# One VectorE operation for the sum of two accumulators and its relu in a seven-product matrix multiplication

## The chip, the core and the metric

The kernel runs on one core of a Trainium2 chip. The metric is the device time of one execution in microseconds (us). The core's engines work side by side, each through its own list of instructions in order: TensorE (PE in the profile, its weight loads PEld), VectorE (DVE), ScalarE (ACT), GpSimd (POOL) and SyncE (SP). They wait for one another by semaphores.

## The reference, cut to what matters

Two layers follow each other: an attention with a squared relu in place of the softmax, over 8 batches, 12 heads, 448 positions and a head size of 64, and then a feed-forward block over the 3584 tokens with width 768 and inner width 2048.

```python
scores = scale * np.matmul(q, k.transpose(0, 1, 3, 2))
attn = np.maximum(scores, 0.0) ** 2 / S
x = np.matmul(attn, v)            # 8 x 448 tokens, 768 wide after the heads are put together
h = x @ w_in                      # 768 -> 2048
g = np.maximum(h, 0.0) ** 2
out = g @ w_out                   # 2048 -> 768
```

## The kernel before, in words

Matrices are fp16 in SBUF, sums are fp32 in PSUM. The batches are taken in four pairs (`pr` 0 to 3). For each pair the kernel makes the attention output `xt`, from it `h` and the squared relu `g`, and from `g` the output. The attention of a later pair is spread in small pieces through the matrix multiplications of an earlier one.

**h, first pair** (batches 0 and 1): plain products, `h_group`, line 414. **h, later pairs** (batches 2 to 7): seven products in place of eight, after Winograd's form of Strassen's method, `h_period`, line 471. A batch is done in two periods (`i0` 0 and 4), so there are 12 periods. A period has two streams `s` of products; the list `order` (lines 528 to 542) gives the 14 products of a period, and beside each what is to be done with its accumulator when its last matmul is issued:

- `copy` (line 486): ScalarE copies an accumulator from PSUM to an fp32 tile in SBUF (`m1`, `m5`, `u2`, `u3`).
- `plus` (line 491): VectorE adds an accumulator in PSUM and such a tile, and writes an fp16 quarter of `g`, 128 partitions x 448 elements. There are 6 in a period, 72 in all (line 493).
- `relu21` (line 502): ScalarE takes the relu of one accumulator into the left half of an upper block of `g`; the right half had been written by `plus`. Then `rest`.
- `c12` (line 506): the last `plus` of a lower block of `g`. Then `rest`.
- `rest` (line 495): puts two VectorE operations on the list `due_g`: a relu in place over what `plus` had written (after `relu21` the right half, 448 elements; after `c12` the whole block, 896 elements; line 498), and the square of the whole block (line 500).

**The output**: `o_groups`, line 610, again by seven products, each of 8 matmuls of 128x384 (line 739), for two rows of tokens at a time. Four of the products take as left operand a sum of parts of `g` that VectorE makes beforehand: `sums`, line 598, `s1` to `s4` (line 608). `s1` and `s2` of the first group are made in the last period of `h` (line 897); `s3` is asked for when the third product ends (`end6`, line 663) and used by the fifth.

**The order of the work.** PE's order is laid down by the list `steps` and by `events`, which bring in pieces of attention (`visit`, line 373) at times of a clock `clock` that adds up the steps' costs (lines 916 to 930). VectorE's order is chosen by a small planner: `at_pe` and `at_ve` are its estimates of how far PE and VectorE are. `due` holds squares of attention tiles, `due_g` the operations of `rest`; each entry has a time from which it may run and a cost. `now_ve` adds the cost of an operation that is issued at once. `fill(until)` issues entries, `due` first, as long as they end by `until`:

```python
def put(d):
    ready, cost, fn, _ = d.popleft()
    at_ve[0] = max(at_ve[0], at_pe[0], ready) + cost
    fn()

def fill(until):
    for d in (due, due_g):
        while d and max(at_ve[0], at_pe[0], d[0][0]) + d[0][1] <= until:
            put(d)
```

`fill` is called at the end of each product in `h` (line 562) and in the output (line 749). `flush_g` (line 365) issues everything on `due_g` up to a batch; it stands ahead of the sums. In the output the entries left over that the next group needs are shared out over the first four products: after product `k` the rounded-up share `some / (4 - k)` of those that are left (lines 745 to 748). The planner's clocks are read by these places alone: neither PE's list nor ScalarE's is ordered by them.

Of the kernel before, what the change touches and what calls it, by code (L numbers as in the profile page):

```python
# [9 lines left out]

# [3 lines left out]
ALU = mybir.AluOpType  # L14
# [3 lines left out]
def kernel(  # L18
# [9 lines left out]
    nc = tc.nc  # L28
# [315 lines left out]
    at_pe = [0.0]  # L344
# [12 lines left out]
# [5 lines that stand above are left out]
    def now_ve(cost, lag=0.25):  # L362
        at_ve[0] = max(at_ve[0], at_pe[0] + lag) + cost
# [38 lines left out]
    def mm_tile(i=None, dtype=FP32):  # L402
        if i is None:
            mm_no[0] += 1
            i = mm_no[0] % len(big)
        return big[i].tile(
            [P, 2048 // mybir.dt.size(dtype)], dtype, name="mm", tag="mm")

    def g_of(b):
        if b // 2 not in gts:  # L410
            gts[b // 2] = g_p.tile([P, NF, 2 * S], FP16, name="g", tag="g")
        return gts[b // 2]
# [58 lines left out]
    def h_period(b, i0, extra):  # L471

        z = (b % 2) * S
        XY = [[None, None], [None, None]]
        keep: dict = {}

        def gs(s, hi, right=None):
            f = i0 + 2 * s + (8 if hi else 0)
            c = (slice(z, z + S) if right is None
                 else slice(z + Q, z + S) if right else slice(z, z + Q))  # L480
            return g_of(b)[:, f:f + 2, c]

        def acc(s, y):
            return XY[s][y][:, 0:S].rearrange("p (r c) -> p r c", r=2)

        def copy(s, y, nm, tag):
            t = late["m"].tile([P, S], FP32, name=nm, tag=tag)
            nc.scalar.activation(out=t, in_=XY[s][y][:, 0:S], func=AF.Copy)
            keep[s, nm] = t.rearrange("p (r c) -> p r c", r=2)

        def plus(s, y, nm, hi, right):
            now_ve(0.54)
            nc.vector.tensor_add(gs(s, hi, right), acc(s, y), keep[s, nm])  # L493

        def rest(g, relu, lag):

            t = at_pe[0] + lag
            due_g.append((t, 0.32 if relu is g else 0.2, lambda: nc.vector.tensor_scalar(  # L498
                out=relu, in0=relu, scalar1=0.0, scalar2=None, op0=ALU.max), b))
            due_g.append((t, 0.54, lambda: nc.vector.tensor_mul(g, g, g), b))  # L500

        def relu21(s):
            nc.scalar.activation(out=gs(s, True, False), in_=acc(s, 0), func=AF.Relu)
            rest(gs(s, True), gs(s, True, True), 0.8)

        def c12(s):
            plus(s, 1, "u2", False, True)
            g = gs(s, False)
            rest(g, g, 0.0)

        def left(k, f, m):

            c, n = f // 4, slice((f % 4) * P, (f % 4 + 1) * P)
            if k in (1, 2):
                return w1[c][:, m + NH * (k - 1), n]
            if k in (4, 7):
                return w1[c + 2][:, m + (NH if k == 4 else 0), n]
            return wsum[{5: 0, 6: 1, 3: 2}[k], c][:, m, n]

        def right(k, m):  # L520
            if k in (1, 2):
                return xts[b][:, m + NH * (k - 1), 0:Q]
            if k in (3, 7):
                return xts[b][:, m + (NH if k == 3 else 0), Q:S]
            return xsum[b, {5: 0, 6: 1, 4: 3}[k]][:, m]


        order = (
            (0, 1, 0, True, lambda: copy(0, 0, "m1", "a")),
            (1, 1, 0, True, lambda: copy(1, 0, "m1", "b")),  # L530
            (0, 2, 1, True, lambda: plus(0, 1, "m1", False, False)),
            (0, 6, 0, False, lambda: copy(0, 0, "u2", "c")),
            (1, 6, 0, False, lambda: copy(1, 0, "u2", "d")),
            (1, 2, 1, True, lambda: plus(1, 1, "m1", False, False)),
            (0, 5, 1, True, lambda: copy(0, 1, "m5", "a")),
            (0, 7, 0, False, lambda: plus(0, 0, "m5", True, True)),
            (1, 7, 0, False, lambda: copy(1, 0, "u3", "b")),
            (1, 5, 1, True, lambda: plus(1, 1, "u3", True, True)),
            (0, 4, 0, False, lambda: relu21(0)),
            (1, 4, 0, False, lambda: relu21(1)),  # L540
            (0, 3, 1, False, lambda: c12(0)),
            (1, 3, 1, False, lambda: c12(1)))

        FREE = {2: 0.6, 5: 0.6, 7: 0.1, 9: 0.6, 12: 0.6, 13: 1.0, 16: 0.6}

        def step(p, r, m):
            s, k, y, fresh, end = order[p]

            def run():
                if fresh and r == 0 and m == 0 and k != 5:  # L550
                    XY[s][y] = mm_tile(s)
                nc.tensor.matmul(  # L552
                    XY[s][y][:, r * Q:(r + 1) * Q],
                    lhsT=left(k, i0 + 2 * s + r, m), rhs=right(k, m),
                    start=(fresh and r == 0 and m == 0), stop=(m == NH - 1),
                    skip_group_check=not (fresh and r == 0))
                if r == 1 and m == NH - 1:
                    end()
                    for fn in extra.get(p, ()):
                        fn()  # L560
                    nx = min(n for n in FREE if n > p)
                    fill(at_pe[0] + (nx - p) * 0.576 + 0.25 + FREE[nx])
            return run

        return [(0.096, step(p, r, m), r == 0 and m == 0 and p not in (0, 1, 6, 8))
                for p in range(14) for r in range(2) for m in range(NH)]
# [393 lines left out]
```

## Time and profile before

| what | value |
|---|---|
| median of 8 runs | 374.06 us (373.76 to 374.51) |
| the profiled execution: its own time | 374.36 us |
| its span, from the first to the last instruction | 372.6 us |
| VectorE busy | 279.2 us (75%), 518 instructions |
| ScalarE busy | 247.7 us (66%), 370 instructions |
| relus of line 498 | 24 of 896 elements, mean 388 ns; 24 of 448, mean 289 ns |
| squares of line 500 | 48 of 896 elements, mean 622 ns |
| sums of line 493 | 72 of 448 elements, mean 620 ns |

A line of the timeline gives the start in us from the span's start, a duration, the engine, the line of the code, the operation with the tile that it writes and those that it reads, the shapes, and how many like it were merged; in brackets stands the idle time before it and what ended that. `mm` is an accumulator in PSUM; `s` is one of the sums `s1` to `s4`; `at` is an attention tile. An instruction's duration is longer than the time that it takes on its engine when the next one is waiting: two squares of attention tiles in a row, each of 0.62 us, are shown merged as 1.15 to 1.16 us. The time that an instruction takes in a full queue is therefore read from start to start.

The stages of the second to fourth pair: `h` from about 121 to 167 us, 210 to 257 and 294 to 331; the output in between and from 331 us to the end. In the 35 us from 296 to 331 VectorE was busy for 29.91 us, ScalarE for 22.04 and PE for all 35.00.

### The profile page before, as it was taken

Reading aid. Unit: us, or ns where it says so; the run is one execution under the profiler, and the core shown is the slowest. Engines: PE = TensorE matmul, PEld = TensorE weight load, DVE = VectorE, ACT = ScalarE, POOL = GpSimd, SP = SyncE. Lnnn points to the kernel's source line nnn. Section 1 sums busy time; section 2 is a strip of 40 time slices with the busy share of each in tenths; the row PEclk is TensorE's granted clock in tenths of the full one; section 3 lists DMA queues with packets and bytes.
Section 4 is the critical chain, followed back from the end, with each engine's and each line's share of the span. In section 5 each row is a group of like instructions: output and inputs, shape, how many; then the busy total and the mean of one; then the engine's idle time right before and its main releaser. Section 6 shows DMA issues by size and latency. Waiting matters only on the chain.

```text
span 372.6 us, 8794 instructions
## 1 busy us (share of the span) xinstructions
PE 361.9 (97%) x3600; PEld 230.8 (62%) x3600; DVE 279.2 (75%) x518; ACT 247.7 (66%) x370; POOL 107.4 (29%) x128
## 2 busy tenths in 40 slices
PE   7889999999999999999999999999999999999994
PEld 3544444445555778885555588786455689975653
DVE  1897677996766887798975668989956688995442
ACT  2997895786667999876556588886665885532220
POOL 8545421747433455522053145140000000000001
PEclk9999999999999999999999999999999999999999
DMA  8999999999999999978799999491233300002333
GB/s 116 199 204 205 205 204 151 122 159 125 206 171 151 174 94 114 113 97 70 132 131 113 187 154 95 79 120 31 52 84 87 86 0 2 2 0 74 95 90 83
DMA packets 121159, 42.64 MB, mean 114 GB/s; under 512 B 100832, under 2 KB 117760, under 8 KB 121120
## 3 DMA queue, kind: packets, MB, share of 16 engines
q0 software_dynamic: 82912, 23.01, 62.0%
q1 hardware_dynamic: 38048, 18.98, 26.8%
q8 instruction: 28, 0.46, 0.5%
q10 hardware_dynamic: 160, 0.10, 0.1%
q14 instruction: 11, 0.09, 0.1%
HBM read 45.61 MB, written 11.01 MB: 152 GB/s over the span
## 4 chain that ended last, share of the span: by engine, by line
PE 84%; DVE 7%; ACT 5%; issue 2%; DMA 1%; POOL 0%; POOLq 0%; DVEq 0%; ACTq 0%
PE mm L739 31%; PE mm L552 25%; PE mm L422 9%; PE slot L254 9%; PE slot L319 7%; ACT at L258 4%; DVE at L371 2%; DMA k<-in_k_dram 1%; DVE s L608 1%; DVE g L500 1%; PE slot L225 1%; DVE g L493 1%; DVE xt L285 1%; DVE osb L646 1%; DVE g L498 1%
## 5 line engine op out<-in xcount | busy, mean ns | idle before, releaser
L258 ACT ACTIVATE at<-slot 128x896 f16<-128x896 f32 x168 | 145.9, 919 | 28.4 <-PE slot L254 28.4
L371 DVE TENSOR_TENSOR at<-at 128x896 f16<-128x896 f16 x168 | 99.1, 619 | 11.1 <-ACT at L258 11.0
L108 POOL DMA_DIRECT2D qs<-in_q_dram x36 | 35.5, 987 | 113.3 <-DMA qT<-qs 106.1
L739 PEld LDWEIGHTS <-s 128*128 128x128 f16 x440 | 41.3, 98 | 34.2 <-DVE s L608 3.8
L254 PE MATMUL slot<-qT,kT 64*64 64x448 f16 x756 | 57.4, 360 | 1.6 <-ACT at L258 0.9
L552 PEld LDWEIGHTS <-w 128*128 128x128 f16 x576 | 54.3, 98 | 5.2 <-issue 4.3
L552 PE MATMUL mm<-xt,w 128*128 128x224 f16 x432 | 49.0, 259 | 0.0
L739 PEld LDWEIGHTS <-g 128*128 128x128 f16 x336 | 31.7, 98 | 24.1 <-issue 4.7
L552 PEld LDWEIGHTS <-ws 128*128 128x128 f16 x432 | 40.3, 98 | 4.7 <-issue 4.7
L739 PE MATMUL mm<-b,g 128*128 128x384 f16 x224 | 40.7, 326 | 0.0
L739 PE MATMUL mm<-b,s 128*128 128x384 f16 x216 | 39.6, 327 | 1.0 <-DVE s L608 0.9
L422 PE MATMUL mm<-xt,w 128*128 128x448 f16 x192 | 39.8, 354 | 0.0
L646 DVE SCALAR_TENSOR_TENSOR osb<-mm,u 128x384 f32<-128x384 f32 (+1 forms) x30 | 16.2, 543 | 31.1 <-ACT u L641 19.2
L739 PE MATMUL mm<-t,s 128*128 128x384 f16 x224 | 39.4, 326 | 0.0
L108 POOL DMA_DIRECT2D ks<-in_k_dram x36 | 35.2, 978 | 12.3 <-DMA b<-in_moe_w_out_dram 5.8
L254 PEld LDWEIGHTS <-kT 64*64 64x64 f16 x756 | 19.6, 104 | 28.9 <-issue 23.9
L575 POOL DMA_DIRECT2D out_dram<-osb x2 | 1.1, 565 | 121.0 <-DVE osb L646 121.0
L641 ACT ACTIVATE u<-mm 128x384 f32<-128x384 f32 x28 | 13.8, 492 | 32.5 <-PE mm L739 31.3
L552 PE MATMUL mm<-x,ws 128*128 128x224 f16 x288 | 34.1, 259 | 0.0
L319 PE MATMUL slot<-at,vt 64*64 64x448 f16 x588 | 31.9, 350 | 0.2
L500 DVE TENSOR_TENSOR g<-g 128x896 f16<-128x896 f16 x48 | 29.8, 622 | 1.2
L493 DVE TENSOR_TENSOR g<-mm,m 128x448 f16<-128x448 f32 x36 | 22.2, 620 | 10.2 <-PE mm L552 7.0
(69 smaller groups left out, 394.9 us busy)
## 6 DMA issues: line engine op xcount, KB each, us to landing
out_dram<-osb SPq DMA_DIRECT2D x52, 192.0 KB, 3.2
vt<-in_v_dram POOLq DMA_DIRECT2D x24, 224.0 KB, 6.5
qs<-in_q_dram POOLq DMA_DIRECT2D x36, 112.0 KB, 4.7
ks<-in_k_dram POOLq DMA_DIRECT2D x36, 112.0 KB, 5.3
w<-in_moe_w_in_dram POOLq DMA_DIRECT2D x8, 384.0 KB, 11.6
b<-in_moe_w_out_dram POOLq DMA_DIRECT2D x4, 768.0 KB, 18.0
q<-in_q_dram POOLq DMA_DIRECT2D x6, 224.0 KB, 7.7
k<-in_k_dram POOLq DMA_DIRECT2D x6, 224.0 KB, 8.2
```

What stands on the lines that cost most here:

```text
L108: nc.gpsimd.dma_start(out=t[:, :, hh, :], in_=heads(src, n)[:, hh].rearrange("p (j d) -> p j d", d=D))
L254: nc.tensor.matmul(ps[c, hh, 0:S], lhsT=kT[r, j, c], rhs=qT[r, :, c], start=True, stop=True)
L258: nc.scalar.activation(out=at, in_=ps[:, :, 0:S], func=AF.Relu, scale=SK)
L319: nc.tensor.matmul(ps[64 * hh:64 * hh + 64, hp, 0:S], lhsT=vt[r, hh, j * D:(j + 1) * D], rhs=at[r, hh, :], start=(j == 0), stop=(j == J - 1))
L371: lambda: nc.vector.tensor_mul(at, at, at), 0))
L422: nc.tensor.matmul(cell[0][:, 0:S], lhsT=w1[f // 4][:, m, (f % 4) * P:(f % 4 + 1) * P], rhs=xts[b][:, m, :], start=(m == 0), stop=(m == NM ...
L493: nc.vector.tensor_add(gs(s, hi, right), acc(s, y), keep[s, nm])
L500: due_g.append((t, 0.54, lambda: nc.vector.tensor_mul(g, g, g), b))
L552: nc.tensor.matmul(XY[s][y][:, r * Q:(r + 1) * Q], lhsT=left(k, i0 + 2 * s + r, m), rhs=right(k, m), start=(fresh and r == 0 and m == 0), ...
L641: nc.scalar.activation(out=t, in_=X[0][:, 0:HALF], func=AF.Copy, scale=CO)
L646: nc.vector.scalar_tensor_tensor(out=osb[row][:, c], in0=acc[0][:, 0:cc.stop - cc.start], scalar=CO, in1=keep[nm][:, cc], op0=ALU.mult, op ...
L739: nc.tensor.matmul(acc[0][:, 0:HALF], lhsT=left()[:, f], rhs=right[:, f], start=(fresh and f == 0), stop=(f == KH - 1), skip_group_check=n ...
```

## The change

`plus` is no longer a plain addition but one VectorE operation that adds, takes the smaller of the sum and 3.4e38, and takes the larger of that and 0: sum and relu at once. As every value that `plus` writes has then had its relu, `rest` puts only the square on `due_g`. The estimated cost of `plus` in the planner stays 0.54, that of the square too; the entries for the relu, of 0.2 and 0.32, are gone.

```diff
+from concourse.dve_ops import TENSOR_ADD_SAT
...
         def plus(s, y, nm, hi, right):
+
             now_ve(0.54)
-            nc.vector.tensor_add(gs(s, hi, right), acc(s, y), keep[s, nm])
-
-        def rest(g, relu, lag):
-
-            t = at_pe[0] + lag
-            due_g.append((t, 0.32 if relu is g else 0.2, lambda: nc.vector.tensor_scalar(
-                out=relu, in0=relu, scalar1=0.0, scalar2=None, op0=ALU.max), b))
-            due_g.append((t, 0.54, lambda: nc.vector.tensor_mul(g, g, g), b))
+            nc.vector._custom_dve(
+                TENSOR_ADD_SAT, out=gs(s, hi, right), in0=acc(s, y),
+                in1=keep[s, nm], s0=3.4e38, s1=0.0)
+
+        def rest(g, lag):
+            due_g.append((at_pe[0] + lag, 0.54,
+                          lambda: nc.vector.tensor_mul(g, g, g), b))
 
         def relu21(s):
             nc.scalar.activation(out=gs(s, True, False), in_=acc(s, 0), func=AF.Relu)
-            rest(gs(s, True), gs(s, True, True), 0.8)
+            rest(gs(s, True), 0.8)
 
         def c12(s):
             plus(s, 1, "u2", False, True)
-            g = gs(s, False)
-            rest(g, g, 0.0)
+            rest(gs(s, False), 0.0)
```

## Prediction

> **What bounds the kernel now.** I read the page first: the span, the engines' busy time and the clock.
>
> ```profile
> span 372.6 us, 8794 instructions
> PE 361.9 (97%) x3600; PEld 230.8 (62%) x3600; DVE 279.2 (75%) x518; ACT 247.7 (66%) x370; POOL 107.4 (29%) x128
> PEclk9999999999999999999999999999999999999999
> ```
>
> PE is busy nearly throughout, at the full clock. VectorE, the only engine that the change touches, has 93 us of idle time in the span. So its busy time is not what the change can save; only places where PE stands still for VectorE are. The second view is therefore the waits of PE from 121 us on, where the seven products of h begin. It has one line:
>
> ```profile
> PE mm L739 <- DVE s L608: 0.9, 2, 0.7
> ```
>
> PE's matmuls waited twice for a sum `s` of VectorE, 0.9 us together, 0.7 the longer. The third view, PE's timeline, shows where:
>
> ```profile
> 261.50 1.47 PE L739 MATMUL mm<-t,s 128*128 128x384 f16 x8
> 263.69 1.47 PE L739 MATMUL mm<-b,s 128*128 128x384 f16 x8 [0.72 <-DVE s L608]
> ```
>
> The bracket counts from the modelled end of the matmul before; what is lost is more. Eight matmuls of this shape that follow each other without a wait take 1.30 us from start to start (337.44 to 338.74 in the same view). The second group was therefore due at 261.50 + 1.30 = 262.80 and came at 263.69: **0.89 us lost**. The other place is the same product of the last pair: 16 such matmuls start at 333.19, the next product was due at 335.79 and came at 336.13: **0.34 us lost**. A further group came late at 207.63 (due 204.66 + 2.60 = 207.26, lost 0.37), behind attention squares that waited for ScalarE; the last relu before it is at 184.7, so the change doesn't reach it. The groups at 130.91 (0.13) and 290.91 (0.2) were late for ScalarE's tiles, not for VectorE's.
>
> The fourth view is VectorE's own timeline ahead of the first of these places:
>
> ```profile
> 257.38 0.38 DVE L498 TENSOR_SCALAR g<-g 128x896 f16<-128x896 f16 x1
> 257.68 0.62 DVE L493 TENSOR_TENSOR g<-mm,u 128x448 f16<-128x448 f32 x1
> 258.21 0.68 DVE L608 TENSOR_TENSOR s<-s,g 128x1024 f16<-128x1024 f16 x1
> 258.81 0.62 DVE L500 TENSOR_TENSOR g<-g 128x896 f16<-128x896 f16 x1
> 259.35 0.27 DVE L498 TENSOR_SCALAR g<-g 128x448 f16<-128x448 f16 x1
> 259.72 0.62 DVE L500 TENSOR_TENSOR g<-g 128x896 f16<-128x896 f16 x1
> 260.27 0.55 DVE L646 SCALAR_TENSOR_TENSOR osb<-mm,m 128x384 f32<-128x384 f32 x1
> 260.73 0.27 DVE L498 TENSOR_SCALAR g<-g 128x448 f16<-128x448 f16 x1
> 261.03 0.63 DVE L500 TENSOR_TENSOR g<-g 128x896 f16<-128x896 f16 x1
> 261.58 0.39 DVE L498 TENSOR_SCALAR g<-g 128x896 f16<-128x896 f16 x1
> 261.88 1.16 DVE L371 TENSOR_TENSOR at<-at 128x896 f16<-128x896 f16 x2
> 262.95 0.69 DVE L608 TENSOR_TENSOR s<-g 128x1024 f16<-128x1024 f16 x1
> ```
>
> No line has a bracket: from 255.77 on VectorE is a full queue, and the sum that PE waits for is its last line. PE's matmul starts 0.74 us after that sum (263.69 - 262.95). Four of the lines ahead of it are relus that the change takes out.
>
> **What is removed.** 48 relus, 16.2 us of busy time (24 x 388 ns + 24 x 289 ns). In the queue above they take, from start to start, 0.30 (257.38), 0.37 (259.35), 0.30 (260.73) and 0.30 (261.58): 1.27 us. The sum then starts at 261.68 at the earliest. One line has another floor: the output sum of L646 at 260.27 needs PE's second product, whose last matmul ends at about 259.76 (258.29 + 1.47); with that the sum starts at about 261.9. It must start by 262.80 - 0.74 = 262.06 for PE not to stand. So the 0.89 us go, with 0.2 to spare. In the last pair VectorE's queue is full from 328.56 to the sum at 335.39; its four relus take 0.37, 0.19, 0.42 and 0.42 us, 1.40 in all, and 0.34 is wanted. That wait goes with 1 us to spare. Everywhere else the relus lie beside PE's matmuls, and their going is worth nothing: PE would have waited for VectorE there, and the view shows that it did not. What is late next is ScalarE: the attention tiles, and the 0.37, 0.2 and 0.13 us above, which I keep.
>
> **What is added.** 72 additions become 72 fused operations. The trace has no such operation, so its price has to be bounded by rows:
>
> ```profile
> L493 DVE TENSOR_TENSOR g<-mm,m 128x448 f16<-128x448 f32 x36 | 22.2, 620 | 10.2 <-PE mm L552 7.0 <-ACT m L488 2.1 <-ACT xt L325 1.0
> L646 DVE SCALAR_TENSOR_TENSOR osb<-mm,u 128x384 f32<-128x384 f32 x28 | 15.6, 556 | 30.9 <-ACT u L641 19.2 <-PE mm L739 11.6
> L646 DVE SCALAR_TENSOR_TENSOR osb<-mm,u 128x192 f32<-128x192 f32 x2 | 0.7, 352 | 0.3 <-PE mm L721 0.3
> ```
>
> L646 does two operations in one pass on the same kinds of source, PSUM and SBUF in fp32. Its two sizes give (556 - 352) / 192 = 1.06 ns an element, so 448 elements would take 556 + 64 x 1.06 = 624 ns; the plain addition takes 620. A second operation in the pass costs nothing there. The lower end is therefore 0 extra (below it nothing: the elements are the same and come from PSUM at the same pace). The upper end is a pass that gains nothing by fusing, the addition plus a relu of 448 elements: 0.19 to 0.37 us extra. I take 0, as the two-operation row is the nearest. At +0.37 the first queue, with two such additions (256.85 and 257.68), keeps 1.27 - 0.74 = 0.53 of its relief, and the second, with three (328.56, 330.80, 331.86), 1.40 - 1.11 = 0.29: together 0.8 in place of 1.2.
>
> [...]
>
> **What is moved.** PE's and ScalarE's orders are not set by the planner's VectorE clock, so only VectorE's own order can change. After the first output product the planner has nine entries left (squares and relus in turn) and issues ceil(9/4) = 3: the lines from 258.81 to 259.72. After the second it issues ceil(6/3) = 2, at 260.73 and 261.03, and `fill` adds one relu. With the relus gone five squares are left: ceil(5/4) = 2, then ceil(3/3) = 1, the same three squares ahead of the sum. But the planner also thinks VectorE freer by the relus' 0.2 and 0.32, and `fill` may bring a further square (0.54 us) ahead of the sum. A square also now waits for ScalarE's relu of the left half with nothing in front of it; where it stands in the same place that only eats saved time.
>
> **The sum.** 0.89 + 0.34 = 1.23 us at best; I take off 0.1 for a queue that is shifted less than counted. From the profiled execution's own 374.36 (span 372.6 and 1.76 around it) that is 373.2; that execution lay 0.30 above the median of 374.06, so the median should be 374.06 - 1.1 = **372.96, say 373.0**. A measurement of this kernel can tell about 0.2%, 0.75 us, from no change.
>
> **Rivals.** First, *more goes than these two waits* (7 in 100): the third late group at 207.63 comes right as well: 1.23 + 0.37 = 1.6 us, 372.5. Against it speaks that no relu stands ahead of it. Second, *one square is brought forward* (10): 1.27 - 0.54 leaves 0.73 of 0.89, less the floor's 0.2; the last pair still gets its 0.34; some 0.85 us, 373.2. Third, *the change hardly does what it says* (27): two squares are brought forward (1.08 us, which eats the first queue's relief) or the fused operation takes 0.1 to 0.4 us more; 0.0 to 0.7 us, 373.4 to 374.0. Fourth, the other side, *VectorE becomes the bound* (18): the fused operation takes far longer. The place is the last h stage, 296 to 331 us: VectorE was busy for 29.91 of 35 us, 5.1 us idle; the 14 relus there took 4.9 us from start to start, and 23 additions stand there. It turns when 23 x extra exceeds 4.9 + 5.1, at an extra of 0.43 us. With an extra of 0.5 that stage alone gives 1.5 us and the queues ahead of the two waits lose what the relus gave: about 375.5; at 0.6 about 378. The rows of L646 speak against it. My forecast itself has 38.
>
> Faster by over 0.2%: 38 + 7 + 10 = 55. Within: 27. Slower: 18. The range runs from 372.2 (the best case and 0.3 for the runs' own spread) to 375.0, which takes in the upper end of the fused operation's price from the rows and the near edge of the fourth case; some 15 in 100 lie above it, a few below.
>
> **What would show it.** The fused operation: 72 instructions with a mean near 620 ns, 0.53 to 0.54 from start to start. No row of L498's kind; VectorE near 263 us busy with 470 instructions. The sum that now starts at 262.95 starts by 262.1, and the matmul behind it has no bracket; the same near 335. The lines of PE up to 261 us at unchanged times. I am wrong if the mean of the fused operation is over 0.8 us, if more squares stand ahead of that sum, or if PE shows new waits for `g`, `m` or accumulators between 121 and 331 us.

## The result and the profile after

The changed kernel takes 372.5 us (median of 10 runs, 372.38 to 373.05), the kernel before in all its runs until then 373.9 us (28 runs, 373.73 to 374.51). The ratio is 0.9962, with a 95% interval of 0.9954 to 0.9970: faster by 1.4 us, between 1.1 and 1.7.

The page of the changed kernel, its span and its engines:

```profile
span 370.7 us, 8742 instructions
PE 360.6 (97%) x3600; PEld 230.6 (62%) x3600; DVE 265.7 (72%) x470; ACT 247.7 (67%) x370; POOL 107.6 (29%) x128
```

VectorE has 48 instructions fewer and 13.5 us less to do; the span is shorter by 1.9 us only. PE's waits from 121 us on, in the changed kernel:

```profile
PE mm L739 <- DVE s L608: 0.2, 1, 0.2
```

Before there were two waits with brackets, of 0.7 us at 263.69 and 0.2 us at 207.63; the late group of the last pair, by 0.34 us, had none. The 0.7 is gone, and the 0.2 that is left is the group near 207 us that the prediction kept. VectorE's timeline at the first place, with the sum in its last line (line 501 is the square, 495 the fused operation, 372 a square of attention tiles):

```profile
256.21 1.15 DVE L495 CUSTOM_DVE_ANT_0 g<-mm,u 128x448 f16<-128x448 f32 x2
257.27 0.68 DVE L608 TENSOR_TENSOR s<-s,g 128x1024 f16<-128x1024 f16 x1
257.87 1.16 DVE L501 TENSOR_TENSOR g<-g 128x896 f16<-128x896 f16 x2
259.22 0.56 DVE L646 SCALAR_TENSOR_TENSOR osb<-mm,m 128x384 f32<-128x384 f32 x1 [0.19 <-issue]
259.70 0.62 DVE L501 TENSOR_TENSOR g<-g 128x896 f16<-128x896 f16 x1
260.23 1.16 DVE L372 TENSOR_TENSOR at<-at 128x896 f16<-128x896 f16 x2
261.30 0.68 DVE L608 TENSOR_TENSOR s<-g 128x1024 f16<-128x1024 f16 x1
```

And PE's:

```profile
260.86 1.48 PE L739 MATMUL mm<-t,s 128*128 128x384 f16 x8
262.17 1.46 PE L739 MATMUL mm<-b,s 128*128 128x384 f16 x8
```

The two groups now stand 1.31 us apart, the pace of matmuls that wait for nothing (1.30 us from 337.44 to 338.74 before); before it was 2.19. Up to this sum the order of VectorE's work is the old one without the relus. In the last pair the group of `b,s` comes 16 matmuls after the start of `t,s`, before:

```profile
333.19 2.84 PE L739 MATMUL mm<-t,s 128*128 128x384 f16 x16
336.13 1.47 PE L739 MATMUL mm<-b,s 128*128 128x384 f16 x8
```

and after:

```profile
331.56 2.76 PE L739 MATMUL mm<-t,s 128*128 128x384 f16 x16
334.17 1.46 PE L739 MATMUL mm<-b,s 128*128 128x384 f16 x8
```

That is 2.61 in place of 2.94 us. The two places make 0.88 + 0.33 = 1.21 us.

A third and smaller place, which the prediction doesn't have, lies in the last h stage, where batch 7 begins. PE and VectorE before, and PE after:

```profile
314.40 1.98 PE L552 MATMUL mm<-xt,w 128*128 128x224 f16 x18
...
314.97 1.15 DVE L493 TENSOR_TENSOR g<-mm,u 128x448 f16<-128x448 f32 x2
```

```profile
312.87 1.89 PE L552 MATMUL mm<-xt,w 128*128 128x224 f16 x18
```

Before, the 18 matmuls took 0.09 us longer. By the single records the 13th of them, the first of product 2 of stream 0, starts at 315.64; at the pace of the others, 0.10 us from start to start, 315.55 was due. It starts afresh in the accumulator that the last `plus` of batch 6's stream 0 reads, and it waits for VectorE's semaphore. That `plus` is the first of the two additions of the row at 314.97, and it ended at 315.59. Two relus of batch 6, at 313.87 and 314.78, stood ahead of it on VectorE's list. In the changed kernel the same addition had ended at 313.52. The row of 18 lasts 1.98 to 2.01 us in the kernel before and in four kernels below that keep batch 6's relus (`fused_relu_kept`, `fused_b5`, `fused_b5_b7`, `before_s3_early`); it lasts 1.89 in the changed kernel and in three below that lack them (`plain_no_relu`, `fused_rest`, `after_s3_early`). No bracket marks this wait. With it the change's part of the trace is 1.30 us.

The other 0.64 us between the two profiled executions lie at the very start. The first product of h begins at 27.46 us in the one and at 26.81 in the other, and every PE line from there up to 261 is earlier by the same 0.63 to 0.65. The first 14 transposes on PE, those of q, took 0.96 us in the one and 0.58 in the other, at a granted clock of 1.00 in both. The next 14, those of k, started at 6.79 in the one and 6.24 in the other, in both behind a wait (0.24 and 0.22 us) that the trace puts down to the transfer of k, and took 0.67 and 0.58. In the profiles of the experiments below the first product of h begins anywhere from 26.80 to 27.37 us, with relus and without. So this part belongs to the execution and not to the change.

### The profile page after: what moved, and what is told of

The parts are those of the page before. It is cut to its first block, busy times and chain, and to the rows that moved or that the text cites. A ratio compares the mean times of both kernels' runs of the same rounds, so it can differ in the third digit from the quotient of the medians.

```text
span 370.7 us, 8742 instructions
## 1 busy us (share of the span) xinstructions
PE 360.6 (97%) x3600; PEld 230.6 (62%) x3600; DVE 265.7 (72%) x470; ACT 247.7 (67%) x370; POOL 107.6 (29%) x128
## 4 chain that ended last, share of the span: by engine, by line
PE 88%; ACT 4%; DVE 3%; issue 1%; DMA 1%; POOL 0%; POOLq 0%; ACTq 0%
PE mm L739 34%; PE mm L552 27%; PE slot L255 10%; PE mm L423 9%; PE slot L320 7%; ACT at L259 4%; DVE at L372 1%; DMA k<-in_k_dram 1%; PE slot L226 1%; DVE xt L286 1%; PE mm L226 0%; DVE kT L217 0%; ACT u L641 0%; DVE osb L646 0%; PE avt L273 0%
## 5 line engine op out<-in xcount | busy, mean ns | idle before, releaser
L646 DVE SCALAR_TENSOR_TENSOR osb<-mm,u 128x384 f32<-128x384 f32 (+1 forms) x30 | 16.2, 543 | 36.2 <-ACT u L641 23.7
L495 DVE CUSTOM_DVE_ANT_0 g<-mm,m 128x448 f16<-128x448 f32 x36 | 22.4, 623 | 15.2 <-PE mm L552 7.6
L501 DVE TENSOR_TENSOR g<-g 128x896 f16<-128x896 f16 x48 | 28.8, 619 | 0.4 <-ACT g L504 0.4
```

Source lines behind the costliest of these rows:

```text
L495: nc.vector._custom_dve(TENSOR_ADD_SAT, out=gs(s, hi, right), in0=acc(s, y), in1=keep[s, nm], s0=3.4e38, s1=0.0)
L646: nc.vector.scalar_tensor_tensor(out=osb[row][:, c], in0=acc[0][:, 0:cc.stop - cc.start], scalar=CO, in1=keep[nm][:, cc], op0=ALU.mult, op ...
```

## The experiments

Line numbers differ from kernel to kernel by what was put in. Theory A: the gain is those two waits of PE, and only relus that stood in the queue ahead of the two sums count. Against it stand: B, the fused operation is itself better than the addition; C, a lighter VectorE helps all along the span. D (the h stages have room for a dearer operation) and E (where that room ends) came up on the way. Each kernel was timed in five rounds against the kernel before, on the same chip.

### The fused operation, with the relus kept

Against the changed kernel, cut to the relu's entry:

```diff
-        def rest(g, lag):
-            due_g.append((at_pe[0] + lag, 0.54,
+        def rest(g, relu, lag):
+            t = at_pe[0] + lag
+            due_g.append((t, 0.32 if relu is g else 0.2, lambda: nc.vector.tensor_scalar(
+                out=relu, in0=relu, scalar1=0.0, scalar2=None, op0=ALU.max), b))
```

> The fused sum and relu is used, and the 48 separate relus stay on VectorE's list as before (they then change no value). Theory A, two waits: the gain of 1.4 us comes from the relus that stood in VectorE's queue ahead of two sums that TensorE waits for; with the relus back both waits are back (0.89 and 0.34 us), and the time is that of before, 373.9 (373.6 to 374.2). Rival B, the fused operation itself is better than the plain addition (shorter, or it releases the accumulators sooner): 372.5 to 373.2. If the fused operation cost more than the addition, over 374.2.

Measured: 373.85 us, ratio 1.000 (0.9991 to 1.0009). PE's waits in this kernel are those of before, to the digit:

```profile
PE mm L743 <- DVE s L612: 0.9, 2, 0.7
```

B falls. The fused operation with a relu behind it costs what the addition with a relu behind it cost.

### The plain addition, without any relu

This kernel leaves out the relu of what `plus` writes; it is there for its time alone.

```diff
-            nc.vector._custom_dve(
-                TENSOR_ADD_SAT, out=gs(s, hi, right), in0=acc(s, y),
-                in1=keep[s, nm], s0=3.4e38, s1=0.0)
+            nc.vector.tensor_add(gs(s, hi, right), acc(s, y), keep[s, nm])
```

> The changed kernel with the plain addition in place of the fused operation, and no relu on what it writes: in batches 2 to 7 this part of the computation is left out, so that the time shows the price of the fused form alone. Theory A, the fused operation costs what the addition costs: the time of the changed kernel, 372.5 (372.3 to 372.8). If the fused form were dearer by 0.05 us in the queues: 0.1 us or so below.

Measured: 372.48 us, ratio 0.9962 (0.9950 to 0.9974), the ratio of the changed kernel to the fourth digit. So the time doesn't tell a fused operation from a plain one. The groups of VectorE in the changed kernel say the same; the mean is the last number ahead of the second bar:

```profile
L495 DVE CUSTOM_DVE_ANT_0 g<-mm,m 128x448 f16<-128x448 f32 x36 | 22.4, 623 | 15.2 <-PE mm L552 7.6 <-ACT m L489 3.9 <-ACT u L489 2.7
L495 DVE CUSTOM_DVE_ANT_0 g<-mm,u 128x448 f16<-128x448 f32 x36 | 22.1, 620 | 8.3 <-PE mm L552 4.2 <-ACT xt L326 2.5 <-ACT u L489 1.6
```

They took 620 ns as plain additions; from start to start it is 0.53 to 0.54 us in both kernels.

### Only batches 5 and 7; all the others; only batch 5

In `h_period`, with `fused = b in (5, 7)`, `b not in (5, 7)` or `b == 5`; against the kernel before, cut:

```diff
+            if not fused:
+                nc.vector.tensor_add(gs(s, hi, right), acc(s, y), keep[s, nm])
+                return
...
+            if not fused:
                 due_g.append((t, 0.32 if relu is g else 0.2, lambda: nc.vector.tensor_scalar(
```

> The change is made for batches 5 and 7 alone (4 of the 12 periods), whose relus stand in the queue ahead of the two sums. Theory A, two waits: 89% of the gain or more, 372.5 to 372.9. Rival C, relief that is spread over the whole span: a third of the gain, 373.4.

> The complement: the change is made for batches 2, 3, 4 and 6 alone (8 of the 12 periods). Theory A, two waits: no gain, 373.9 (373.6 to 374.1), and both waits of TensorE for the sum as before. Rival C, spread relief: two thirds of the gain, 373.0.

> The change is made for batch 5 alone, whose relus stand ahead of the first of the two sums. Theory A, two waits that add up: 0.89 us and what goes with it, but the 0.34 us of the last pair stay: 372.9 (372.8 to 373.1). If a wait that is taken away early came back later as another: 373.5 to 373.9.

Measured: batches 5 and 7, a third of the relus, 372.58 us, ratio 0.9965 (0.9953 to 0.9978). The other two thirds, 373.85, ratio 1.000 (0.9991 to 1.0009). Batch 5 alone, 373.01, ratio 0.9975 (0.9965 to 0.9985). PE in the kernel with batches 5 and 7:

```profile
261.41 1.48 PE L747 MATMUL mm<-t,s 128*128 128x384 f16 x8
262.73 1.46 PE L747 MATMUL mm<-b,s 128*128 128x384 f16 x8
```

and in its complement:

```profile
261.17 1.47 PE L747 MATMUL mm<-t,s 128*128 128x384 f16 x8
263.35 1.48 PE L747 MATMUL mm<-b,s 128*128 128x384 f16 x8 [0.71 <-DVE s L616]
```

In the first the group of `b,s` follows in 1.32 us, in the second in 2.18, as before the change. C falls: 32 of the 48 relus are worth nothing that the time shows, where its interval leaves some 0.3 us. By the trace the complement does take out the 0.09 us of the third place (its 18 matmuls take 1.89 us), which the time can't tell. Batch 5 alone brings 0.88 us by the medians, 0.6 to 1.3 by the interval, where the queue's 0.89 was expected, and the last pair's wait is still there (331.69 to 334.64 in its PE timeline: 2.95 us). So the two waits add up, and what is won early is not lost again later.

### The sum asked for earlier, without and with the change

```diff
             def end2():
                 new_osb()
                 plus(0, c0, "m1")
+                ahead(3)
...
             def end6():
                 copy("u2")
-                ahead(3)
```

> The kernel before, with all its relus and plain additions; only the sum s3 is asked for one product earlier (after the output sum of the second product in place of after the third). Theory A, two waits: the sum is ahead of the queue, both waits go without any relu being removed (1.2 us), and the third late group at 207.63 us, whose s3 stood behind attention squares that waited for ScalarE, goes too (0.37 us): 372.2 to 372.7. Rival C, spread relief: VectorE has as much to do as before, 373.9.

> The changed kernel, and s3 asked for one product earlier as well. Theory A: the two waits can go only once; of the 1.6 us that the earlier sum gave alone only the third group's 0.37 us is left to win: 372.1 (372.0 to 372.3), the same as the earlier sum alone gave with all relus in place (372.24). Rival C, that the lighter load on VectorE is worth something by itself: below 371.8, down to 370.9 if both gains add.

Measured: on the kernel before, 372.24 us, ratio 0.9956 (0.9943 to 0.9968); on the changed kernel, 372.24, ratio 0.9954 (0.9942 to 0.9967). In neither has PE any wait from 121 us on that the view would list. VectorE's queue in the first of the two, with all its relus:

```profile
259.26 0.55 DVE L646 SCALAR_TENSOR_TENSOR osb<-mm,m 128x384 f32<-128x384 f32 x1
259.73 1.15 DVE L371 TENSOR_TENSOR at<-at 128x896 f16<-128x896 f16 x2
260.80 0.68 DVE L608 TENSOR_TENSOR s<-g 128x1024 f16<-128x1024 f16 x1
261.40 0.27 DVE L498 TENSOR_SCALAR g<-g 128x448 f16<-128x448 f16 x1
261.70 0.62 DVE L500 TENSOR_TENSOR g<-g 128x896 f16<-128x896 f16 x1
```

The sum has changed places with a relu, a square and another relu, and that alone does it: 1.57 us by the medians of that set, where 0.89 + 0.34 + 0.37 = 1.60 were expected. The third late group is on time as well: near 207 us its 16 matmuls take 2.62 us from start to start, where they took 2.97. Once the sum is ahead, the change adds nothing that the time shows. This is the strongest of the experiments: one moved call does at least what 48 instructions taken away do. By the medians both kernels lie some 0.3 us below the changed one, about what the third group is worth, but the intervals of the ratios overlap.

### A dearer fused operation

How much could the fused operation have cost? Four kernels put something behind each of the 72: the same operation over 64 or 192 of its elements into a spare tile, the same again over half the elements, or all of it again. The diffs are those of 64 elements and of half.

```diff
+            nc.vector._custom_dve(
+                TENSOR_ADD_SAT,
+                out=zeros[:, 0:64].rearrange("p (r c) -> p r c", r=2),
+                in0=acc(s, y)[:, :, 0:32], in1=keep[s, nm][:, :, 0:32],
+                s0=3.4e38, s1=0.0)
```

```diff
-            nc.vector._custom_dve(
-                TENSOR_ADD_SAT, out=gs(s, hi, right), in0=acc(s, y),
-                in1=keep[s, nm], s0=3.4e38, s1=0.0)
+            for n in (2, 1):
+                nc.vector._custom_dve(
+                    TENSOR_ADD_SAT, out=gs(s, hi, right)[:, 0:n],
+                    in0=acc(s, y)[:, 0:n], in1=keep[s, nm][:, 0:n],
+                    s0=3.4e38, s1=0.0)
```

> The changed kernel, with each fused operation done twice in a row (the second writes the same values again). This puts 0.53 us more on VectorE for each of the 72, as a fused operation at half the pace would. By the fourth rival of the prediction, which turns at 0.43 us, VectorE becomes the bound in the h stages: the last one is over by 23 x 0.53 - 10.0 = 2.2 us, the one before by 0.5, and both waits for the sum are back: 375.5 to 377.5. Rival D, that only the two waits count and the h stages have room: 373.9 to 374.5.

> The changed kernel, with each fused operation followed by a second one over the first half of its elements (224 of 448, the same values again): some 0.30 us more for each of the 72. By the prediction's reckoning 23 x 0.30 = 6.9 us is less than the 10.0 us of room in the last h stage, so no new bound; the first queue keeps 1.27 - 0.60 = 0.67 us of its relief, so that a wait of 0.2 to 0.4 us is back, and the second none: 372.7 to 373.0. Rival, that TensorE's accumulators are held too long well before VectorE is full: over 373.9.

> The changed kernel; each fused operation is followed by a second one over 64 of its elements, which writes to a spare tile that nobody reads. That puts some 0.14 us more on VectorE for each of the 72 (an estimate from 1.06 ns an element and some 0.07 us for the instruction). Theory E, new: the h stages turn at about 0.2 us, since an extra of 0.42 us cost 10.7 us and one of 0.66 us 23.3, a line that meets zero at 0.22: no new bound, 372.5 to 372.9. The reckoning of the prediction (turns at 0.43): the same, 372.5 to 372.7. If there is no threshold and each addition's extra is paid: 372.5 + 72 x 0.14 = 382.

> As the run with 64 elements, with 192: some 0.27 us more for each of the 72. Theory E (turns at about 0.2 us, then 52 us for each us of extra): 375 (373.9 to 376.5), with waits of TensorE for accumulators in the h stages. The reckoning of the prediction by average room: no new bound, one wait of 0.3 us back, 372.8.

The extra per addition is read from start to start of the pair, less the 0.54 of one:

| kernel | extra, us | time, us | ratio to before |
|---|---|---|---|
| changed | 0 | 372.5 | 0.9962 (0.9954 to 0.9970) |
| with 64 elements | 0.13 | 372.94 | 0.9977 (0.9968 to 0.9986) |
| with 192 | 0.26 | 376.2 | 1.0069 (1.0056 to 1.0082) |
| with half | 0.42 | 383.24 | 1.0248 (1.0234 to 1.0262) |
| with all | 0.65 | 395.76 | 1.0582 (1.0567 to 1.0596) |

The two larger ones put more on VectorE than their expectations reckoned (0.42 and 0.65 in place of 0.30 and 0.53): the second operation writes what the first wrote and started 0.65 us after it, where two independent ones start 0.54 apart. Even so the reckoning by room is refuted: both came out far above what it gave. At 0.42 us, about the point where the prediction saw the turn, the kernel is 10.7 us behind the changed one; at 0.26, 3.7 us. D falls with it; what came is the rival that the run with half had beside it, accumulators held too long well before VectorE is full: in that run PE waited for the fused operation 3.4 us in 8 places of h, while VectorE was busy for 44.99 of 49, 46.40 of 52 and 35.40 of 39 us in the three h stages. E, which set the turn near 0.2 from the two larger runs, expected 375 with 192 elements and got 376.2, inside its range; with 64 it expected at most 372.9 and got 372.94, where a wait of PE is already seen. Its line is a rough one, since the slope rises all the way (25, 44 and 54 us for each us of extra between the last four rows).

Where it happens is seen in the kernel with 64 elements, in the last h stage. These are VectorE and PE; line 495 is the fused operation, 498 the operation put in:

```profile
315.73 0.62 DVE L495 CUSTOM_DVE_ANT_0 g<-mm,m 128x448 f16<-128x448 f32 x1
315.73 0.74 PE L557 MATMUL mm<-xt,w 128*128 128x224 f16 x6
316.26 0.21 DVE L498 CUSTOM_DVE_ANT_1 zeros<-mm,m 128x64 f16<-128x64 f32 x1
...
316.53 0.73 PE L557 MATMUL mm<-x,ws 128*128 128x224 f16 x6
```

The six matmuls of `x,ws` are product 5 of stream 0. It starts afresh in the accumulator that product 2 filled (line 550 takes no new tile for it), so it must wait until VectorE has read that. Six such matmuls take 0.57 to 0.58 us without a wait; here 0.80 lie between the two groups, 0.22 more, and the group starts 0.06 us after the operation put in has ended at 316.47. In the changed kernel the fused operation at this place ended at 315.96 and the group started at 316.31, unhindered. With 192 elements PE's view of waits has:

```profile
PE mm L557 <- DVE zeros L498: 0.6, 2, 0.5
PE mm L744 <- DVE s L613: 0.6, 2, 0.4
```

and with all elements twice, where line 496 is the fused operation:

```profile
PE mm L553 <- DVE g L496: 12.6, 25, 1.3
```

## Why the prediction was right, point by point, and where it was not

- **What bounds the kernel.** Right: PE, and VectorE only where PE stands for it (the complement: ratio 1.000). The reading of the view was too trusting: the second of its two waits is the group at 207.63, which stays, and not the last pair, whose 0.34 us it doesn't list. So it could not show that PE never stood for VectorE elsewhere, and the 0.09 us in the last h stage were such a place.
- **The two waits.** Right in place and size: 0.89 and 0.34 us expected, 0.88 and 0.33 won by the trace of after, 0.88 for batch 5 alone and 1.2 for batches 5 and 7 by their medians. The 0.1 us that was taken off for a shifted queue was not needed.
- **The floor and the spare time.** Right: the sum starts at 261.30, which is 1.01 us earlier once the 0.64 of the start is taken off, and not the whole 1.27 of the four relus. 0.19 us were lost ahead of L646. The prediction had set a floor of 0.2 there and named PE's product for it; the view says issue, but L646 starts 0.10 us after the modelled end of that product (257.65 + 1.47), as at 340.92, where it starts 0.09 after its product's end and the view names PE. PE needed the sum by 262.17 - 0.74 = 261.43, so 0.13 us were to spare.
- **The planner.** Right: the same three squares stand between the second and the third sum; none was brought forward.
- **The price of the fused operation.** Right: 620 and 623 ns, as the two-operation row of L646 had it (624 ns for 448 elements, by its two sizes). 448 elements took no longer than in the plain addition, 620 ns.
- **What is kept.** Right: the late group near 207 us is late by the same 0.37, and the two that wait for ScalarE's tiles are as late as before: the one near 130 came at 130.27 in place of 130.91, earlier by the 0.64 of the start alone, and the one near 291 starts 0.81 us after the six matmuls ahead of it, 0.80 before.
- **The time.** 373.0 was forecast, 372.5 measured. The forecast before rounding, 372.96, was high by 0.46: 0.16 of it is the median of before, 374.06 by the first runs and 373.9 by all, 0.13 is what was taken off the 1.23, and 0.09 is the third place. By the three places the median would be 373.9 - 1.30 = 372.6; the interval of 1.1 to 1.7 holds the 1.3. The lines of PE up to 261 us were to stay at their times; all had moved by 0.64. That was the start of the profiled execution of before, 374.36, which lay in the upper part of its runs. Only the median is to be compared, as the prediction did.
- **The fourth rival, and the bound on the price.** Here a step failed: "It turns when 23 x extra exceeds 4.9 + 5.1, at an extra of 0.43 us", and with it the 0.8 us of gain that the prediction still saw at +0.37. The runs put the turn between 0.13 and 0.26. The step that failed is to count the stage's 5.1 us of idle time as room for the additions. In the kernel before, VectorE's listed waits in that stretch are 4.3 us: 1.6 for accumulators that PE had not finished and 2.7 for tiles of ScalarE. PE in turn must have its accumulators read soon after: it lost 0.22 us at the group of 316.53 with 64 elements, and with all elements twice it waited 12.6 us in 25 places. So in these runs that idle time could not be filled with work that belongs to the chain itself. (Also, the relus' 4.9 us from start to start hold 0.7 us of short idle times that the 5.1 hold too; that alone would move the turn only to 0.40.) Had the fused operation been dearer by the upper end of the rows, 0.37 us, the change would have been slower: between 376.2 and 383.2, by the runs at 0.26 and 0.42, outside the stated range. The forecast took 0, from the two-operation row, and so didn't rest on this step.

What is not settled is the last 0.1 us of the median, which is less than the interval. What sets the pace of PE's first transposes and the time at which k lands was not tried.

## What to carry to other kernels

Taking instructions off an engine that isn't the bound was worth here what it took out of the queues ahead of the results, and of the reads of accumulators, that the bounding engine was waiting for, and nothing measurable elsewhere. Look for those few places first, single records included, since a view of waits can leave short ones out (0.34 and 0.09 us here), and asking for a result earlier can win as much without touching the work (1.57 us here, against 1.4). When you price an operation in a chain of two engines that wait for each other's buffers, go by the spare time of each step from one engine to the other, not by the idle time of a stage: the latter made an operation look safe up to 0.43 us that was harmful at 0.26.

## What the runs showed of the hardware

- A fused operation of sum, minimum and maximum over 448 elements, from PSUM and SBUF in fp32 to fp16, took 620 to 623 ns, a plain addition 620 ns; from start to start both 0.53 to 0.54 us. The same over 192 elements took 348 ns.
- Two fused operations in a row started 0.53 to 0.54 us apart when independent, and 0.65 us apart when the second wrote what the first had written.
- PE's matmul into an accumulator started 0.05 to 0.06 us after the end of the VectorE operation that it waited for (315.59 to 315.64 in the kernel before, 316.47 to 316.53 in the one with 64 elements).
- The first 14 transposes on PE took 0.58 us in one profiled execution, 0.96 in another and 0.78 in a third, with the same program up to there; the granted clock was 1.00 there in the first two, and 0.998 in the mean over the third's span. The 0.78 moved nothing behind it: the first matmuls of the scores started at 7.56 us, against 7.55 with 0.58. With 0.96, and k's transposes behind its transfer 0.55 us later, they started at 8.19, and all that follows was later by that 0.64 us, half of what the change is worth.
